# Attention with a threshold mask, followed by an MLP: keys and queries transposed in float32 before they are split in two, not after

## The chip, the cores and the metric

The kernel runs on one core of a Trainium2 chip. The metric is the device time of one execution in microseconds (us). A core has a matrix engine (TensorE, PE in the profile, with its weight loads as PEld), a vector engine (VectorE, DVE), an engine for activation functions and copies (ScalarE, ACT), a general engine (GpSimd, POOL) and an engine that here issues all transfers (SyncE, SP). Each engine runs its own instructions in a fixed order and waits for the others by semaphores.

## The reference

```python
def _attn_ref(q, k, v, tau):                       # 8 batches, 8 heads, 576 tokens, 64 dims
    scores = scale * np.matmul(q, k.transpose(0, 1, 3, 2))
    thresh = np.max(scores, axis=-1, keepdims=True) - tau
    scores = np.where(scores >= thresh, scores, -1000000000.0)
    attn = np.exp(scores - np.max(scores, axis=-1, keepdims=True))
    attn = attn / (np.sum(attn, axis=-1, keepdims=True) + 1e-09)
    return np.matmul(attn, v).astype(np.float32)

def _moe_ref(x, w_in, w_out):                      # x: 4608 tokens x 512, d_ff 2048
    h = x @ w_in
    g = np.maximum(h, 0.0) + np.log1p(np.exp(-np.abs(h)))      # softplus
    return (g @ w_out).astype(np.float32)
```

The heads of the attention's output are put side by side (8 x 64 = 512) and go through the MLP. The two weight matrices arrive in float64.

## The kernel before, in words

**Two halves of a number.** Matrix products are made in a shorter float format, `fp32r`. Every operand is split in two: `hi`, the value rounded to `fp32r` (`hi_of`), and `lo`, what is left of it (`lo_of`, a subtraction; L124). A product is then made of three or four products of halves. Much of what POOL, ACT and DVE do is this splitting.

**Units and tiles.** The attention goes by units of one head pair of one batch. A tile is 128 query rows of one head against its 576 keys; tile `M` holds the last 64 rows of both heads. Batches 1 to 7 have four units of nine tiles each (kind "all", 28 units). Batch 0 is cut into units of four tiles (kind "one") and of five (kind "two"), so that the MLP can begin early; there are eight of these. In all there are 36 units and 288 tiles. For a tile the steps are: scores (L391), row maximum on DVE (L397), exponential on ACT (L405), mask and row sum on DVE (L410), transposes of the masked weights `e_all` on PE (L441), their hi copy on ACT (L462) and lo on DVE (L124, `gL`), and the product with the values (L485 and after).

**What prepares a unit.** While a unit's tiles run, the steps of `pre` make the next unit ready; `ST` (and `STEPS` for batch 0) says at which tile each is called. Before the change these are: `split_k` and `split_q` make hi and lo of the loaded keys and queries on POOL (L117 hi, L124 lo), side by side as 128 columns, 64 of hi and 64 of lo. `qkT` transposes each block of 128 tokens in `fp32r` on PE (L336 for the eight whole blocks of the two heads, L328 and L330 for the last 64 tokens), so that one transpose gives hi on 64 partitions and lo on the other 64. ACT copies the results from PSUM: `kT` (L340), `qT` with the scale (L349), the rest (L358, L364). Two transfers on SP make `qT` with its halves swapped (L353, L354). A score product is `kT` with `qT` plus `kT` with the swapped `qT`, which gives all four products of halves. `split_v` makes the values' halves on POOL (`vt`).

**The MLP.** It runs in chunks of tokens between the attention's tiles, one chunk of 512 tokens to a batch, as single matmuls that fill TensorE's queue: hidden layer `h` (L574, L576, L578), softplus on ACT (L596, `st`), hi on DVE (L121, `g`) and lo on POOL (L124, `g<-st,g`), output `o` (L632, L634, L636; the last takes the lo half). Sixteen blocks `g_<chunk>_<block>` make a chunk. After the last tile, at about 1340 us, only the MLP is left.

**The weights.** In batch 0 and after it the float64 weights are loaded, decoded with integer operations on DVE (six for a block, L172 to L184), two on ACT and one on POOL (L189), and the decoded `w_in` goes to a store in HBM. There are 32 blocks.

**What sets the order.** The program calls each tile's steps by a fixed pattern, a planner's list of late calls (`defer`, `point`) puts copies a step or two behind, and a scheduler then fixes the order of each engine's instructions. All transfers are on SP's queue.

## Time and profile before

| | |
|---|---|
| median of 3 runs | 1544.3 us (1540.53 to 1549.28) |
| profiled execution: its time / its span | 1545.64 us / 1543.5 us |
| mean granted TensorE clock | 0.966 |
| PE, PEld busy | 91%, 78% of the span |
| DVE, ACT, POOL busy | 70%, 59%, 38% |
| work only in the MLP | from about 1340 us |

The page divides the span into busy shares and follows back the chain of work that ended last. The first 250 us, in which the weights are decoded, and the time behind them differ in what they wait for, so the table's shares are to be read by stretches of time. Of an operation the page gives its line, its engine, the names of its tiles (out<-in), its partitions by elements, its count, its total busy time and the mean of one in ns, and behind the second bar the idle time of the engine just ahead of it, with what ended it.

### The profile page before, as it was taken

To read this page: it belongs to the slowest core of one execution; us is meant where nothing else is said; L and a number is where in the kernel's file an instruction comes from. 1 tells how busy PE (TensorE), PEld (TensorE's weight loads), DVE (VectorE), ACT (ScalarE), POOL (GpSimd) and SP (SyncE) were. 2 spreads that over 40 slices of the span, in tenths; PEclk is the share of its full clock that TensorE was granted. 3 is DMA by queue.
4 is the path that set the end of the run, shared out by engine and by line. 5 is a ranking of instruction groups with operands and counts; after the bars stand their busy time and mean duration, and the time that the engine had idled before them with its cause. 6 is when DMAs were issued, how large, how long until landed. Compare 5 with 4: busy or idle time off the path is not lost.

```text
span 1543.5 us, 24467 instructions
## 1 busy us (share of the span) xinstructions
PE 1410.7 (91%) x8076; PEld 1202.7 (78%) x8076; DVE 1073.9 (70%) x2372; ACT 917.8 (59%) x1861; POOL 588.1 (38%) x612
## 2 busy tenths in 40 slices
PE   4555778889899999999999999999999999999998
PEld 4444767778788888888888888888888888878887
DVE  7999798778777777777777777777777777511212
ACT  5565676677576657666776576666666666511110
POOL 4554445334243334334433433344334332242321
PEclk9776899999999999999999999999999999999999
DMA  6767764544343355434443353335334532352331
GB/s 171 217 184 207 244 204 133 172 132 127 106 126 113 108 130 144 116 112 118 149 115 104 100 160 102 108 110 147 111 106 114 146 105 77 101 173 96 118 101 41
DMA packets 142030, 202.44 MB, mean 131 GB/s; under 512 B 38192, under 2 KB 97872, under 8 KB 141904
## 3 DMA queue, kind: packets, MB, share of 16 engines
q1 hardware_dynamic: 141904, 200.89, 44.6%
q8 instruction: 64, 1.05, 0.3%
q14 instruction: 62, 0.51, 0.1%
HBM read 152.44 MB, written 27.41 MB: 117 GB/s over the span
## 4 chain that ended last, share of the span: by engine, by line
PE 61%; ACT 10%; DVE 8%; issue 4%; DMA 3%; POOL 2%; SPq 1%; POOLq 0%; ACTq 0%; DVEq 0%
PE s L391 8%; PE o L636 6%; PE o L632 6%; PE o L634 6%; PE h L574 6%; PE s L441 6%; PE h L576 6%; PE h L578 6%; PE pv L485 3%; PE pv L486 3%; ACT L596 2%; DVE e_all L410 2%; ACT gH L462 2%; ACT st L596 2%; ACT L405 1%
## 5 line engine op out<-in xcount | busy, mean ns | idle before, releaser
L124 POOL TENSOR_TENSOR g<-st,g 128x512 fp32r<-128x512 f32 x144 | 193.2, 1359 | 206.3 <-DVE g L121 206.3
L410 DVE SCALAR_TENSOR_TENSOR e_all<-s,thr,e_all 128x576 f32<-128x576 f32 x288 | 234.7, 816 | 34.8 <-ACT e_all L405 29.6
L576 PE MATMUL h<-xl,wi 128*128 128x512 f32 (+1 forms) x640 | 246.4, 385 | 0.0
L574 PE MATMUL h<-xh,wi 128*128 128x512 f32 (+1 forms) x640 | 244.4, 382 | 1.1 <-DMA wi<-wi_d 0.5
L578 PE MATMUL h<-xh,wi 128*128 128x512 f32 (+1 forms) x640 | 242.8, 379 | 0.0
L397 DVE TENSOR_REDUCE negm<-s 128x1 f32<-128x576 f32 x288 | 216.9, 754 | 29.6 <-PE s L391 25.6
L636 PE MATMUL o<-wo_o,g 128*128 128x512 f32 x576 | 231.6, 402 | 4.9 <-POOL g L124 4.9
L632 PE MATMUL o<-wo_o,g 128*128 128x512 f32 x576 | 233.5, 405 | 1.7 <-ACT st L596 1.4
L634 PE MATMUL o<-wo_o,g 128*128 128x512 f32 x576 | 229.6, 399 | 0.0
L405 ACT ACTIVATE e_all<-s,negm 128x576 f32<-128x576 f32 x288 | 214.0, 743 | 7.8 <-DVE negm L397 5.9
L391 PE MATMUL s<-kT,qT 128*128 128x288 f32 x1024 | 201.1, 317 | 5.1 <-DMA qT<-qT 2.1
L124 DVE TENSOR_TENSOR gL<-s,gH 128x512 fp32r<-128x512 f32 (+1 forms) x240 | 150.2, 634 | 74.5 <-ACT gH L465 38.9
L462 ACT CAST gH<-s 128x512 fp32r<-128x512 f32 (+1 forms) x240 | 129.0, 550 | 120.5 <-PE s L446 65.6
L391 PEld LDWEIGHTS s<-kT,qT 128*128 128x128 f32 x1024 | 153.6, 196 | 23.8 <-DVE gH L124 14.7
L121 DVE CAST g<-st 128x512 fp32r<-128x512 f32 x144 | 67.0, 502 | 149.5 <-ACT st L596 148.9
L485 PE MATMUL pv<-gH,vt 128*128 128x320 f32 (+1 forms) x512 | 148.4, 310 | 1.4 <-ACT gH L462 1.4
L596 ACT ACTIVATE st<-h 128x512 f32<-128x512 f32 x144 | 78.5, 596 | 117.8 <-PE h L578 117.1
L486 PE MATMUL pv<-gL,vt 128*128 128x320 f32 (+1 forms) x512 | 146.1, 305 | 0.0
L574 PEld LDWEIGHTS h<-xh,wi 128*128 128x128 f32 x640 | 123.9, 194 | 22.5 <-ACT gH L462 0.7
L441 PE MATMUL s<-identr,e_all 128*128 128x128 f32 x864 | 135.2, 279 | 6.9 <-DVE e_all L410 5.9
L578 PEld LDWEIGHTS h<-xh,wi 128*128 128x128 f32 x640 | 123.2, 193 | 19.4
L576 PEld LDWEIGHTS h<-xl,wi 128*128 128x128 f32 x640 | 123.8, 193 | 18.6
(107 smaller groups left out, 2558.9 us busy)
## 6 DMA issues: line engine op xcount, KB each, us to landing
wi<-wi_d SPq DMA_DIRECT2D x160, 512.0 KB
qT<-qT SPq DMA_DIRECT2D x112, 128.0 KB
kn<-in_k_dram SPq DMA_DIRECT2D x36, 256.0 KB
qn<-in_q_dram SPq DMA_DIRECT2D x36, 256.0 KB
vn<-in_v_dram SPq DMA_DIRECT2D x36, 256.0 KB
wc_i<-in_moe_w_in_dram SPq DMA_DIRECT2D x16, 512.0 KB
wc_o<-in_moe_w_out_dram SPq DMA_DIRECT2D x16, 512.0 KB
R<-r_d SPq DMA_DIRECT2D x56, 144.0 KB
```

Source lines behind the costliest of these rows:

```text
L124: eng.tensor_tensor(out=out_, in0=in_, in1=hi.bitcast(F32), op=ALU.subtract)
L391: nc.tensor.matmul(sp[:, hf, 0:HS], lhs, s.kT[j][:, k0 + hf * HS:k0 + (hf + 1) * HS], start=(m == 0), stop=(m == len(parts) - 1))
L397: nc.vector.reduce_max(negm, s.sp[t][:, :, 0:HS], axis=AX.XY, negate=True)
L405: nc.scalar.activation(e_all[:, s.half[t], :].rearrange("p (h n) -> p h n", h=2), s.sp[t][:, :, 0:HS], AF.Exp, bias=s.m[t][0], scale=1.0)
L410: nc.vector.scalar_tensor_tensor(out=e2, in0=s.sp[t][:, :, 0:HS], scalar=s.m.pop(t)[1], in1=e2, op0=ALU.is_ge, op1=ALU.mult, accum_out=s.s ...
L441: nc.tensor.transpose(main[:, c, :], e[:, c0:c0 + P], ident)
L574: nc.tensor.matmul(h, wi[:, 0, cc, :], u.h[cc], start=(cc == 0), stop=False)
L576: nc.tensor.matmul(h, wi[:, 0, cc, :], u.l[cc], start=False, stop=False)
L578: nc.tensor.matmul(h, wi[:, 1, cc, :], u.h[cc], start=False, stop=(cc == NCC - 1))
L632: nc.tensor.matmul(o, gh[:, sl], wo[fc][:, 0, :], start=(i == 0), stop=False)
L634: nc.tensor.matmul(o, gh[:, sl], wo[fc][:, 1, :], start=False, stop=False)
L636: nc.tensor.matmul(o, gl[:, sl], wo[fc][:, 0, :], start=False, stop=(i == QF - 1))
```

## The change

Keys and queries go to TensorE as they were loaded, in float32. One transpose takes two blocks of 64 columns, which are two of the four token blocks of a head (`pair_T`), so the eight whole blocks of a head pair need four transposes for keys and four for queries, with the identity read as float32. The last 64 tokens of both heads, keys in 64 partitions and queries in the others, are loaded into a tile of their own, `rn`, and share one transpose (`rest_T`). The result has no halves yet: on partitions 0 to 63 stand the columns of one token block, on 64 to 127 those of the other.

In unit 0 ACT makes hi and DVE lo directly from PSUM (`pair_parts`). In every other unit (`pair_raw`) ACT copies the raw values, 128x256 of keys and 128x256 of queries (128x128 in batch 0's "one" and "two"), into the tile `raw`, and POOL makes hi and lo from it, each on 64 partitions: for each head two hi and two lo of `kT`, and two of each for `qT`. The lo goes to the other 64 partitions, as a score product needs it. The rests are copied to `rr` by ACT and split by POOL in the same way (`rest_raw`, `rest_parts`), with those for tile `M` in `qm`. The swapping transfers follow POOL's last instruction. The steps of `pre` become six and are called later in the unit: tiles 3, 4, 4, 5, 6 and 8 in place of 1, 3, 4, 4, 5, 6, 6 and 8. Transposes of keys and queries fall from 648 to 308 (19 to 9 for a unit "all"); POOL's instructions rise from 617 to 944, SP's fall from 923 to 823 and ACT's from 1704 to 1673.

```diff
-ST = (1, 3, 4, 4, 5, 6, 6, 8)
+ST = (3, 4, 4, 5, 6, 8)
...
+RAW = ("all", "one", "two")
...
+                s.cc = (slice(0, 2), slice(0, 1), slice(1, 2))[("all", "one", "two").index(kind)]
...
+        s.rn = apool.tile([P, 2, D], F32, tag="rn", bufs=2, name=f"rn_{s.i}")
+        for n, (t, src) in enumerate(((s.kn, k), (s.qn, q))):
             load_rows(s, t, src)
-            if t is s.qn and s.kind == "one":
-                continue
-            for j in range(2):
-                nc.sync.dma_start(t[j * SR:(j + 1) * SR, NC, :], src[s.b, h0 + j, SM:S, :])
+            nc.sync.dma_start(s.rn[n * SR:(n + 1) * SR], src[s.b, h0:h0 + 2, SM:S, :].rearrange("h p d -> p h d"))
+        s.kT, s.qT, s.vt = [], [], []
...
-    def split_k(s):
-        s.k2 = apool.tile([P, 9, 2 * D], F32R, tag="k2", bufs=1, name=f"k2_{s.i}")
-        hi_of(s.eng, s.k2[:, :, 0:D], s.kn[:, 0:9, :])
-        lo_of(s.eng_lo, s.k2[:, :, D:2 * D], s.kn[:, 0:9, :], s.k2[:, :, 0:D])
-        s.q2, s.kT, s.qT, s.vt = [], [], [], []
-    def split_q(s, j):
-        t = apool.tile([P, NC + 1, 2 * D], F32R, tag="q2", bufs=1, name=f"q2_{s.i}_{j}")
-        a, z = s.cols.start, s.cols.stop
-        if j == 0 and s.kind != "one":
-            z += 1
-        qj = s.qn[:, j * (NC + 1) + a:j * (NC + 1) + z, :]
-        hi_of(s.eng, t[:, a:z, 0:D], qj)
-        lo_of(s.eng_lo, t[:, a:z, D:2 * D], qj, t[:, a:z, 0:D])
-        s.q2.append(t)
...
-    def qkT(s, j, n):
-        ps = ps_g.tile([P, 512], F32, tag="g", name=f"tr_{s.i}_{j}_{n}")
-        pr = ps.bitcast(F32R)
-        if n == 2:
-            nc.tensor.transpose(pr[:, 0:P], s.k2[:, NC, :], identr)
-            if j == 0 and s.kind != "one":
-                nc.tensor.transpose(pr[:, P:2 * P], s.q2[0][:, NC, :], identr)
-            defer(1, lambda: qkT_rest(s, j, ps))
-            return
-        cols = range(NC) if n == 0 else range(NC)[s.cols]
-        for c in cols:
-            src = s.k2[:, j * (NC + 1) + c, :] if n == 0 else s.q2[j][:, c, :]
-            nc.tensor.transpose(pr[:, c * P:(c + 1) * P], src, identr)
-        if n == 0:
-            s.kT.append(apool.tile([P, S + SR], F32R, tag="kT", name=f"kT_{s.i}_{j}"))
-            t = s.kT[j]
-            defer(1, lambda: nc.scalar.copy(t[:, SR:S], ps))
-        else:
-            t = [apool.tile([P, SM], F32R, tag=f"qT{i}", name=f"qT{i}_{s.i}_{j}") for i in range(2)]
-            s.qT.append(t)
-            w = slice(cols[0] * P, (cols[-1] + 1) * P)
-            defer(1, lambda: queries(t[0][:, w], t[1][:, w], ps[:, w]))
-    def queries(t0, t1, ps):
-        nc.scalar.activation(t0, ps, AF.Copy, scale=qscale)
-        swap(t0, t1)
-    def swap(t0, t1):
-        nc.sync.dma_start(t1[0:D].bitcast(F32), t0[D:P].bitcast(F32))
-        nc.sync.dma_start(t1[D:P].bitcast(F32), t0[0:D].bitcast(F32))
-    def qkT_rest(s, j, ps):
-        nc.scalar.copy(
-            s.kT[j].rearrange("p (k n) -> p k n", n=SR)[:, 0:NC * 2 + 2:NC * 2 + 1, :],
-            ps[:, j * SR:(j + 1) * SR].unsqueeze(1).to_broadcast([P, 2, SR]),
-        )
+    def pair_T(s, j):
+        ps = ps_g.tile([P, 4, P], F32, tag="g", name=f"tr_{s.i}_{j}")
+        for i, t in enumerate((s.kn, s.qn)):
+            for c in range(2) if i == 0 else range(2)[s.cc]:
+                a = (j * (NC + 1) + 2 * c) * D
+                nc.tensor.transpose(ps[:, 2 * i + c, :], t.rearrange("p s d -> p (s d)")[:, a:a + P], ident)
+        s.kT.append(apool.tile([P, S + SR], F32R, tag="kT", name=f"kT_{s.i}_{j}"))
+        s.qT.append([apool.tile([P, SM], F32R, tag=f"qT{i}", name=f"qT{i}_{s.i}_{j}") for i in range(2)])
+        defer(1, lambda: pair_raw(s, j, ps) if s.i and s.kind in RAW else pair_parts(s, j, ps))
+    def blocks(t, c, o):
+        return t.rearrange("p (c o n) -> p c o n", o=2, n=P)[:, c, o, :]
+    def half(i):
+        return slice(i * D, (i + 1) * D)
+    def pair_raw(s, j, ps):
+        t = apool.tile([P, 4, P], F32, tag="raw", bufs=1, name=f"raw_{s.i}_{j}")
+        nc.scalar.copy(t[:, 0:2, :], ps[:, 0:2, :])
+        q_ = slice(2 + s.cc.start, 2 + s.cc.stop)
+        nc.scalar.activation(t[:, q_, :], ps[:, q_, :], AF.Copy, scale=qscale)
+        for i, c, to in ((0, slice(0, 2), s.kT[j][:, SR:S]), (2, s.cc, s.qT[j][0])):
+            for o in range(2):
+                src = t[half(o), i + c.start:i + c.stop, :]
+                hi = blocks(to[half(o)], c, o)
+                hi_of(nc.gpsimd, hi, src)
+                lo_of(nc.gpsimd, blocks(to[half(1 - o)], c, o), src, hi)
+        swap(s, j)
+    def pair_parts(s, j, ps):
+        t0 = s.qT[j][0]
+        for o in range(2):
+            src = ps[half(o), 2 + s.cc.start:2 + s.cc.stop, :]
+            hi = blocks(t0[half(o)], s.cc, o)
+            nc.scalar.activation(hi, src, AF.Copy, scale=qscale[half(o)])
+            nc.vector.scalar_tensor_tensor(out=blocks(t0[half(1 - o)], s.cc, o), in0=src, scalar=qscale[half(o)],
+                                           in1=hi.bitcast(F32), op0=ALU.mult, op1=ALU.subtract)
+        swap(s, j)
+        for o in range(2):
+            src = ps[half(o), 0:2, :]
+            to = s.kT[j][:, SR:S]
+            hi = blocks(to[half(o)], slice(0, 2), o)
+            nc.scalar.copy(hi, src)
+            lo_of(nc.vector, blocks(to[half(1 - o)], slice(0, 2), o), src, hi)
+    def swap(s, j):
+        t0, t1 = s.qT[j]
+        w = slice(s.cols.start * P, s.cols.stop * P)
+        for o in range(2):
+            nc.sync.dma_start(t1[half(o), w].bitcast(F32), t0[half(1 - o), w].bitcast(F32))
+    def rest_T(s):
+        ps = ps_g.tile([P, 512], F32, tag="g", name=f"re_{s.i}")
+        nc.tensor.transpose(ps[:, 0:P], s.rn.rearrange("p h d -> p (h d)"), ident)
+        s.rr = apool.tile([P, P], F32, tag="rr", bufs=1, name=f"rr_{s.i}")
+        defer(1, lambda: rest_raw(s, ps))
+    def rest_raw(s, ps):
+        nc.scalar.copy(s.rr[:, 0:SR], ps[:, 0:SR])
+        nc.scalar.activation(s.rr[:, SR:P], ps[:, SR:P], AF.Copy, scale=qscale)
+        defer(1, lambda: rest_parts(s, 0))
+    def rest_parts(s, j):
+        def sides(t):
+            return t.rearrange("p (k n) -> p k n", n=SR)[:, 0:NC * 2 + 2:NC * 2 + 1, :]
+        src = s.rr[half(j), 0:SR].unsqueeze(1).to_broadcast([D, 2, SR])
+        hi = sides(s.kT[j][half(j)])
+        hi_of(nc.gpsimd, hi, src)
+        lo_of(nc.gpsimd, sides(s.kT[j][half(1 - j)]), src, hi)
         if j == 0 and s.kind != "one":
             for m in range(2):
-                nc.scalar.activation(qm[:, 0, m, m * SR:(m + 1) * SR], ps[:, P + m * SR:P + (m + 1) * SR],
-                                     AF.Copy, scale=qscale)
-            swap(qm[:, 0], qm[:, 1])
+                src, w = s.rr[half(m), SR:P], half(m)
+                hi = qm[half(m), 0, m, w]
+                hi_of(nc.gpsimd, hi, src)
+                lo_of(nc.gpsimd, qm[half(1 - m), 0, m, w], src, hi)
+            for o in range(2):
+                nc.sync.dma_start(qm[half(o), 1].bitcast(F32), qm[half(1 - o), 0].bitcast(F32))
...
-    def pre(s, first_):
-        def a():
-            split_k(s)
-        def b():
-            split_q(s, 0)
-            qkT(s, 0, 0)
-        def c():
-            qkT(s, 0, 1)
-            split_v(s, 0)
-        def d():
-            split_v(s, 1)
-            split_q(s, 1)
-        return [a, b, lambda: qkT(s, 0, 2), c, d, lambda: qkT(s, 1, 0), lambda: qkT(s, 1, 1),
-                lambda: qkT(s, 1, 2)]
-    STEPS = {
-        ("all", "all"): ST,
-        ("one", "one"): (0, 0, 0, 1, 1, 2, 2, 3),
-        ("one", "two"): (0, 0, 0, 1, 1, 2, 2, 3),
-        ("two", "two"): (0, 0, 1, 1, 2, 3, 3, 4),
-        ("two", "one"): (0, 0, 1, 1, 2, 3, 3, 4),
-        ("two", "all"): (0, 0, 1, 1, 2, 3, 4, 9),
-    }
+    def pre(s):
+        return [lambda: pair_T(s, 0), lambda: rest_T(s), lambda: split_v(s, 0), lambda: split_v(s, 1),
+                lambda: pair_T(s, 1), lambda: rest_parts(s, 1)]
+    STEPS = {"all": ST, "one": (0, 0, 1, 1, 2, 3), "two": (1, 1, 2, 2, 3, 4)}
...
-    eng, u0.eng, u0.eng_lo = u0.eng, nc.scalar, nc.vector
-    split_k(u0)
-    split_q(u0, 0)
-    for n in (0, 2, 1):
-        qkT(u0, 0, n)
-        point()
+    pair_T(u0, 0)
+    rest_T(u0)
+    point()
     load_v(u0)
     load(units[1])
-    split_q(u0, 1)
-    for n in (0, 2, 1):
-        qkT(u0, 1, n)
-        point()
-    u0.eng, u0.eng_lo = eng, nc.gpsimd
+    pair_T(u0, 1)
+    point()
+    rest_parts(u0, 1)
```

How the order moves on two engines, first on POOL where unit 29's keys and queries are prepared, around the lo halves of the MLP's blocks `g_5_14` and `g_5_15`. Before:

```order
L522 TENSOR_TENSOR xp_11522<-xp_11522,R_11950 128x576
L124 TENSOR_TENSOR g_5_14_12043<-st_14_12032,g_5_14_12042 128x512
L124 TENSOR_TENSOR g_5_15_12047<-st_15_12030,g_5_15_12046 128x512
L117 TENSOR_SCALAR q_29_1_12175<-qn_11849 128x4x64
L124 TENSOR_TENSOR xl_2_12212<-xst_2_12094,xh_2_12211 128x512
L124 TENSOR_TENSOR q_29_1_12175<-qn_11849,q_29_1_12175 128x4x64
```

With the change (`raw_0` and `rr` are ACT's raw copies, `kT_0` and `qT_29_0` the unit's transposed keys and queries):

```order
L550 TENSOR_TENSOR xp_11588<-xp_11588,R_12018 128x576
L125 TENSOR_SCALAR kT_0_12124<-raw_0_12131 64x2x128 x2
L132 TENSOR_TENSOR kT_0_12124<-raw_0_12131,kT_0_12124 64x2x128
L132 TENSOR_TENSOR g_5_14_12111<-st_14_12100,g_5_14_12110 128x512
L132 TENSOR_TENSOR g_5_15_12115<-st_15_12098,g_5_15_12114 128x512
L132 TENSOR_TENSOR kT_0_12124<-raw_0_12131,kT_0_12124 64x2x128
L125 TENSOR_SCALAR qT_29_0_12125<-raw_0_12131 64x2x128 x2
L132 TENSOR_TENSOR qT_29_0_12125<-raw_0_12131,qT_29_0_12125 64x2x128 x2
L125 TENSOR_SCALAR kT_0_12124<-rr_12188 64x2x64
```

Two hi and one lo of `kT_0` now stand between `xp` and `g_5_14`, where nothing stood. The same is found in the chunks 2, 3, 4 and 6.

The same engine in batch 0, where unit 2 (kind "one") is prepared. Before:

```order
L117 TENSOR_SCALAR q_2_0_457<-qn_400 128x2x64
L124 TENSOR_TENSOR q_2_0_457<-qn_400,q_2_0_457 128x2x64
L117 TENSOR_SCALAR k_2_454<-kn_399 128x9x64
L124 TENSOR_TENSOR k_2_454<-kn_399,k_2_454 128x9x64
L117 TENSOR_SCALAR vt_0_517<-vn_405 128x5x64
L124 TENSOR_TENSOR vt_0_517<-vn_405,vt_0_517 128x5x64
L189 TENSOR_TENSOR wa_i_2_413<-wa_i_2_413 128x512
L117 TENSOR_SCALAR q_2_1_523<-qn_400 128x2x64
L124 TENSOR_TENSOR q_2_1_523<-qn_400,q_2_1_523 128x2x64
L117 TENSOR_SCALAR vt_1_520<-vn_405 128x5x64
L124 TENSOR_TENSOR vt_1_520<-vn_405,vt_1_520 128x5x64
```

With the change:

```order
L125 TENSOR_SCALAR vt_0_528<-vn_411 128x5x64
L132 TENSOR_TENSOR vt_0_528<-vn_411,vt_0_528 128x5x64
L125 TENSOR_SCALAR kT_0_463<-raw_0_482 64x2x128 x2
L132 TENSOR_TENSOR kT_0_463<-raw_0_482,kT_0_463 64x2x128 x2
L125 TENSOR_SCALAR qT_2_0_464<-raw_0_482 64x128 x2
L132 TENSOR_TENSOR qT_2_0_464<-raw_0_482,qT_2_0_464 64x128 x2
L125 TENSOR_SCALAR kT_0_463<-rr_468 64x2x64
L132 TENSOR_TENSOR kT_0_463<-rr_468,kT_0_463 64x2x64
L125 TENSOR_SCALAR kT_1_589<-rr_468 64x2x64
L132 TENSOR_TENSOR kT_1_589<-rr_468,kT_1_589 64x2x64
L197 TENSOR_TENSOR wa_i_2_419<-wa_i_2_419 128x512
L125 TENSOR_SCALAR vt_1_531<-vn_411 128x5x64
```

Before, two instructions split the keys of both heads and two the queries of a head. With the change one head's keys and queries take eight and the last keys of both heads four, all behind the values `vt_0`; the other head's eight follow further down. `wa_i` is a block of weights.

On TensorE at unit 29's preparation, with the MLP's `o` matmuls between them. Before:

```order
L636 MATMUL o_3_0_12026<-wo_o_2518,g_5_14_12043 128x512
L632 MATMUL o_3_0_12026<-wo_o_2593,g_5_15_12046 128x512
L634 MATMUL o_3_0_12026<-wo_o_2593,g_5_15_12046 128x512
L636 MATMUL o_3_0_12026<-wo_o_2593,g_5_15_12047 128x512
L634 MATMUL o_3_1_12097<-wo_o_2373,g_5_13_11716 128x512
L636 MATMUL o_3_1_12097<-wo_o_2373,g_5_13_11717 128x512
L632 MATMUL o_3_1_12097<-wo_o_2518,g_5_14_12042 128x512
L328 MATMUL tr_0_2_12107<-identr,k_29_11940 128x128
L330 MATMUL tr_0_2_12107<-identr,q_29_0_12051 128x128
L336 MATMUL tr_0_1_12110<-identr,q_29_0_12051 128x128 x4
```

With the change:

```order
L664 MATMUL o_3_0_12094<-wo_o_2549,g_5_14_12111 128x512
L660 MATMUL o_3_0_12094<-wo_o_2630,g_5_15_12114 128x512
L662 MATMUL o_3_0_12094<-wo_o_2630,g_5_15_12114 128x512
L664 MATMUL o_3_0_12094<-wo_o_2630,g_5_15_12115 128x512
L662 MATMUL o_3_1_12176<-wo_o_2387,g_5_13_11785 128x512
L664 MATMUL o_3_1_12176<-wo_o_2387,g_5_13_11786 128x512
L660 MATMUL o_3_1_12176<-wo_o_2549,g_5_14_12110 128x512
L370 MATMUL re_12186<-identr,rn_11923 128x128
L419 MATMUL s_141<-kT_1_11827,qT_28_1_11828 128x288 x2
```

One transpose of `rn` stands where there were one of the last keys, one of the last queries and four of the queries; the first head's queries are transposed earlier, two at a time, together with its keys.

11 lines of the change are left out of this document (2 added, 9 removed).

## The prediction

> **What bounds the kernel now.** I read the page's busy shares and slices first, then the busy time by stretches, to learn where a saved microsecond of an engine counts. The columns of the second fence are start and end, length, then busy time and count on PE, PEld, DVE, ACT and POOL, granted clock, DMA share and GB/s.
>
> ```profile
> PE 1410.7 (91%) x8076; PEld 1202.7 (78%) x8076; DVE 1073.9 (70%) x2372; ACT 917.8 (59%) x1861; POOL 588.1 (38%) x612
> PE   4555778889899999999999999999999999999998
> DVE  7999798778777777777777777777777777511212
> ```
>
> ```profile
> 0.00:250.00 250.00, 152.74 (x896) 137.67 (x897) 222.42 (x443) 161.32 (x360) 127.03 (x146) 0.81 0.66 201
> 32.00:51.00 19.00, 11.44 (x73) 9.91 (x71) 17.54 (x39) 13.40 (x33) 10.79 (x15) 0.84 0.70 201
> 74.00:98.00 24.00, 11.86 (x73) 10.71 (x72) 23.45 (x45) 16.79 (x40) 13.86 (x18) 0.74 0.53 161
> 250.00:400.00 150.00, 134.74 (x915) 118.31 (x913) 113.67 (x249) 105.14 (x242) 56.44 (x63) 0.99 0.48 135
> 900.00:950.00 50.00, 49.77 (x292) 42.12 (x291) 36.23 (x84) 36.07 (x68) 19.35 (x20) 1.00 0.39 116
> ```
>
> Two regimes show. From 250 us on PE bounds: it is busy for 49.77 of 50 us at 900, with DVE and ACT at 36 and POOL at 19. In the first 250 us PE is busy for 153 and DVE for 222, because DVE decodes weights beside the masks of batch 0. So fewer transposes pay only in the 28 units "all" behind it, and what slows DVE costs in front.
>
> **PE's transposes.** The groups give a transpose's own duration; as PE overlaps matmuls, what one costs is the spacing in the chain of waits (start, time on the chain, instructions).
>
> ```profile
> L336 PE MATMUL tr<-identr,k 128*128 128x128 f32 x288 | 35.9, 252 | 9.9 <-DVE identr L94 6.9 <-POOL k L124 2.9
> L441 PE MATMUL s<-identr,e_all 128*128 128x128 f32 x864 | 135.2, 279 | 6.9 <-DVE e_all L410 5.9
> ```
>
> ```profile
> 904.21 0.44 PE s L441 x4
> ...
> 916.78 0.29 PE tr L336 x4
> ...
> 920.47 0.06 PE tr L328
> 920.53 0.06 PE tr L330
> 920.59 0.08 PE tr L336
> ...
> 921.34 0.20 PE tr L336 x3
> ```
>
> Four `fp32r` transposes take 0.28 to 0.29 us, 0.07 each, and those of the rests 0.06. The new ones read float32 with the float32 identity, as those of `e_all` do: 0.44 for four, 0.11 each. Per unit before: four groups of four, 2x0.29 + 2x0.28, and three rests, 3x0.06, make 1.32 us for 19. After: 9x0.11 = 0.99. That is 0.33 us a unit, and 28 units make **-9.2 us**. Half as many transposes at 1.6 times the price save a quarter of their time, not half. Bounds: -5 if batch 1 is still held by DVE and a fresh float32 transpose costs 0.12, -12 if it costs 0.10.
>
> **The lo of the MLP's g.** POOL's queue is where the change adds most, so I looked at where PE waits for POOL now: before `o` L636, whose lo half POOL makes.
>
> ```profile
> L124 POOL TENSOR_TENSOR g<-st,g 128x512 fp32r<-128x512 f32 x144 | 193.2, 1359 | 206.3 <-DVE g L121 206.3
> L636 PE MATMUL o<-wo_o,g 128*128 128x512 f32 x576 | 231.6, 402 | 4.9 <-POOL g L124 4.9
> ```
>
> Most of `g` has slack: POOL idles ahead of it and PE's idle time before L636 is 4.9 us in all. In each chunk one pair has none. This is the place of the order fence, in a chunk near 1040 us (start, duration, engine, line, operation, tile; in brackets the idle time before).
>
> ```profile
> 1035.44 1.43 POOL L522 TENSOR_TENSOR xp<-xp,R 128x576 f32<-128x576 f32 x1 [1.54 <-DMA R<-r_d]
> ...
> 1036.66 1.09 ACT L596 ACTIVATE st<-h 128x512 f32<-128x512 f32 x2
> ...
> 1037.64 0.59 ACT L340 CAST kT<-tr 128x512 fp32r<-128x512 f32 x1
> ...
> 1038.29 2.64 POOL L124 TENSOR_TENSOR g<-st,g 128x512 fp32r<-128x512 f32 x2 [1.42 <-DVE g L121]
> ...
> 1039.74 0.50 PE L636 MATMUL o<-wo_o,g 128*128 128x512 f32 x1 [0.51 <-POOL g L124]
> ...
> 1040.98 0.50 PE L636 MATMUL o<-wo_o,g 128*128 128x512 f32 x1 [0.27 <-POOL g L124]
> ```
>
> ```profile
> L117 POOL TENSOR_SCALAR q<-qn 128x256 fp32r<-128x256 f32 x28 | 11.4, 407 | 25.2 <-PE tr L336 24.7
> L124 POOL TENSOR_TENSOR q<-qn,q 128x256 fp32r<-128x256 f32 x28 | 20.7, 738 | 1.9
> L117 POOL TENSOR_SCALAR q<-qn 128x128 fp32r<-128x128 f32 x10 | 3.5, 346 | 15.9 <-PE tr L336 15.8
> L124 POOL TENSOR_TENSOR q<-qn,q 128x128 fp32r<-128x128 f32 x10 | 4.7, 471 | 0.8
> L462 ACT CAST gH<-tm 128x256 fp32r<-128x256 f32 x16 | 5.2, 375 | 7.2 <-PE tm L441 7.2
> ```
>
> POOL sits idle for 1.42 us ahead of these `g`, and PE already waits for them. In the new order two hi and one lo of `kT_0` come between. They need ACT's raw copy, which takes the place of the `kT` copy at 1037.64: 128x256 instead of 128x512, so 0.38 us, to 1038.02. POOL then does 2x0.407 + 0.738 = 1.55 us and begins `g` at 1039.57 instead of 1038.29: 1.28 us later, and PE with it. Five chunks have this order: **+6.4 us**. I price the 64-partition operations by their columns, not their elements: no row has 64 partitions on POOL, and 256 against 128 columns is 738 against 471. Bounds: 0, if the copy comes sooner because the transposes no longer wait for a split; 5x2.3 = 11.5, if the second lo and the scheduler's other pairs are in the way as well.
>
> **DVE's decoding beside a busier POOL.** POOL's load per unit: "one" had 0.721 + 1.490 for keys and 2x(0.346 + 0.471) for queries, 3.85 us.
>
> ```profile
> L117 POOL TENSOR_SCALAR k<-kn 128x576 fp32r<-128x576 f32 x35 | 25.2, 721 | 158.9 <-PE tr L328 158.8
> L124 POOL TENSOR_TENSOR k<-kn,k 128x576 fp32r<-128x576 f32 x35 | 52.1, 1490 | 2.7
> L189 POOL TENSOR_TENSOR wa_i<-wa_i 128x512 fp32r<-128x512 f32 x16 | 21.3, 1333 | 10.8 <-DVE wa_i L184 4.2 <-ACT e_all L405 3.6 <-ACT thr L399 3.0
> ```
>
> Now it has 4x(0.407 + 0.738) for keys, 4x(0.346 + 0.471) for queries and half as much, 1.63, for the rests: 9.5 us, 5.6 more. "Two" gains some 7, with the two pairs for `qm`. Three units of "one" and four of "two" (unit 0 takes the other path) make about 42 us on POOL's 127 of the first 250 us. Does DVE feel it? The same decode operation on the same size:
>
> ```profile
> 13.28 1.93 POOL L124 TENSOR_TENSOR k<-kn,k 128x576 fp32r<-128x576 f32 x1
> ...
> 13.97 1.52 DVE L184 TENSOR_SCALAR wa_i<-wb_i 128x512 uint32<-128x512 uint32 x1
> ...
> 27.77 0.42 DVE L184 TENSOR_SCALAR wa_i<-wb_i 128x512 uint32<-128x512 uint32 x1
> ```
>
> ```profile
> L184 DVE TENSOR_SCALAR wa_o<-wb_o 128x512 uint32<-128x512 uint32 x13 | 8.5, 656 | 0.1
> L184 DVE TENSOR_SCALAR wa_i<-wb_i 128x512 uint32<-128x512 uint32 x16 | 8.3, 519 | 0.0
> ```
>
> Under POOL's subtraction it took 1.52 us and ended behind it, without one 0.42. The mean excess is 0.10 and 0.24 us in the two groups, 4.7 us for 29 blocks; six such kinds of operation make 28 us now. Scaled by 42/127 that is 9.3 us, of which DVE's busy share there, 0.89, reaches the end: **+8 us**. Bounds: 0, if the new operations fall into its waits; for the top, 42 us times the share of time in which DVE decodes, 192 operations at some 0.6 us or nearly half of 250, 20 us. The Trainium skill says in "SBUF — State Buffer" (two separate sides) that GpSimd and certain DVE operations, those with two SBUF inputs among them, lock a shared port pair for a whole instruction, and the other blocks. The 1.52 us agrees with it; taken for every overlap, the rule would put the bound of 20 in the sum, where the means of the groups speak for 8.
>
> **What costs nothing.** ACT copies less per unit and bounds nowhere (36 of 50 us, 161 of 250), so I count no gain. POOL's 7.7 us more per unit "all" lie in its idle 31 of 50 us, except at the `g` above; without that cover they would show as PE waiting before `o`. Unit 0 makes its parts on ACT and DVE with no split ahead of the transposes; its eight short DVE operations replace two long ones while the first weights are awaited, and I call it even, within 1.5 us. On SP the waits of the loads for `k2`'s buffers go:
>
> ```profile
> SPq L286 <- POOL k L124: 143.6, 26, 8.2
> ```
>
> but the two swapping transfers now wait for POOL's last lo of the queries, and behind them in SP's order stand the loads of the MLP's weights `wi`, which have three buffers. A unit "all" calls its last `pair_T` at tile 6 of 9, with two tiles of time; I count nothing. In batch 0 the units are shorter and the margin is thin, which is a rival.
>
> **The sum.** -9.2 + 6.4 + 8 = +5.2 us on the profiled 1545.6 (span 1543.5) gives 1550.8. The profiled run lies 1.3 above the median of 1544.3, so 1549.5 for a median: **1549 us**, no change. About 0.5% (7.7 us) is what a measurement of this kernel can tell from none. The likeliest case's own range is 1541 to 1558.
>
> **Rivals.** *Faster.* The `kT` copies come early enough, or the hi of `g` late enough, that POOL's wait costs nothing, and decoding does not feel the new operations. For it: the 206 us of idle time ahead of `g`, and new work that is spread over the unit. Against: it waits at that very place and PE behind it. Only the transposes remain: 1545.6 - 9.2 - 1.3 = 1535 us.
>
> *Slower: POOL ends last in batch 0.* In the two stretches quoted POOL works 10.79 of 19 us ("one") and 13.86 of 24 ("two"); with 5.6 and 7 more it is at 16.4 of 19 and 21 of 24, in an order fixed ahead, with waits for ACT's raw copies, for DVE's decoded blocks (L189, 1.333 us each) and for values. The second head's eight instructions follow all these; when two blocks or so stand ahead of them, keys and queries are 2.7 us late, PE's first scores of the next unit wait, and DVE with them. It decides from the point where POOL's work with its waits passes the unit's length. Seven units make 19 us: 1549.5 + 19 = 1568 us. Against: 86% is not full.
>
> *A transpose costs its whole duration.* "TensorE: Matmul & The Clock Gate" (Part 4) of the Trainium skill gives about 275 ns for a transpose in context, mostly latency, which would make their number count. By this case's rows that is 28x(19x0.252 - 9x0.279) = 64 us, and 1549.5 - 64 + 9 = 1495 us. The spacing of 0.06 to 0.11 us in the chain speaks against it.
>
> **Chances.** No change 0.38; faster 0.31 and whole durations 0.04, so 0.35 faster; POOL's lateness 0.27 slower, as it takes little to use up a thin margin. The range runs from between the fast case and the one below it to the slow one with the decode bound: 1526 to 1570.
>
> **What would show it.** Right: the chain has four float32 transposes at 0.44 us; POOL starts those `g` over a us later and PE's idle time before `o` L636 <- POOL grows from 5 to about 11 us; decode operations on DVE grow by some 30% of their excess and batch 0 ends 8 us later. Wrong: PE waits for `kT` or `qT` before scores L391 in units 1 to 8 (POOL's lateness); no growth before `o` (the fast case); spacing of 0.25 us per transpose.

## The result, and the profile after

| | before | changed |
|---|---|---|
| median | 1542.4 us (1540.4 to 1549.3, 4 runs) | 1591.4 us (1589.0 to 1593.5, 4 runs) |
| ratio | | 1.0309, 95% interval 1.0271 to 1.0347 |
| span of the profiled run | 1543.5 us | 1587.1 us |
| mean granted TensorE clock | 0.966 | 0.945 |

The change makes the kernel 3.1% slower, 49 us. The forecast was no change, 1549 us, with a range up to 1570. The two profiled runs, in which the places below are read, took 1545.64 and 1588.98 us, so they show 43 of the 49 us; the rest is spread between runs and is not placed.

Where it goes is read from the first mask of each unit, taken from the order of the mask operations on DVE (us from the span's start):

| first mask of unit | 1 | 2 | 4 | 6 | 8 | 13 | 21 | 29 | 35 |
|---|---|---|---|---|---|---|---|---|---|
| before | 34.1 | 54.7 | 103.3 | 163.5 | 231.8 | 419.5 | 738.5 | 1059.4 | 1299.8 |
| changed | 35.0 | 62.2 | 119.0 | 192.7 | 275.1 | 465.7 | 783.2 | 1103.8 | 1344.1 |
| later by | 0.9 | 7.5 | 15.7 | 29.3 | 43.3 | 46.3 | 44.7 | 44.5 | 44.3 |

The whole loss lies in batch 0 (units 0 to 7) and the first units behind it: 43.3 us by unit 8, of which unit 8 itself wins 4.9 back (40.0 us instead of 44.9), and 7.8 us more in units 9 to 12 (150.7 us instead of 142.9). From unit 13 on nothing is lost and a little is won: a chunk of four units takes 160.3 us instead of 160.4 (three chunks from unit 20 to unit 32).

The page's busy shares of the changed kernel, and its stretches (columns as in the prediction):

```profile
PE 1408.9 (89%) x7736; PEld 1189.3 (75%) x7736; DVE 1093.2 (69%) x2377; ACT 880.1 (55%) x1798; POOL 838.0 (53%) x1234
```

```profile
0.00:250.00 250.00, 132.93 (x677) 118.69 (x677) 204.82 (x389) 133.21 (x308) 161.19 (x247) 0.74 0.60 176
900.00:950.00 50.00, 47.90 (x268) 40.30 (x267) 37.70 (x87) 26.48 (x57) 26.05 (x40) 0.97 0.43 119
```

POOL has 838 us of work instead of 588, in 1234 instructions instead of 612 by the two pages; the count of 944 given with the change is too low. In the first 250 us it is busy for 161, not 127, and DVE, which bound that stretch with 222 us, is busy for only 205: it has work and doesn't get to it. What it waits for stands in the waits of DVE in the first 275 us (total, times, longest), before:

```profile
DVE negm L397 <- PE s L391: 7.4, 7, 3.7
DVE wa_i L172 <- DMA wc_i<-in_moe_w_in_dram: 3.9, 1, 3.9
```

and in the changed kernel, with SP's longest wait of the same stretch:

```profile
DVE wa_o L180 <- DMA wc_o<-in_moe_w_out_dram: 14.5, 8, 4.5
DVE wa_i L180 <- DMA wc_i<-in_moe_w_in_dram: 10.3, 4, 4.1
```

```profile
SPq L365 <- POOL qT L132: 76.9, 17, 8.3
```

DVE now waits 24.8 us for weights to be decoded, where it was 4.4 before, and SP stands for 76.9 us in front of the swapping transfers, until POOL has made its last lo of the queries (before the change the longest sum there was 14.4 us, for ACT's copy). A place where the two meet, from the timeline of the changed kernel:

```profile
99.14 0.60 SPq L290 DMA_DIRECT2D rn<-in_q_dram  x1
...
103.32 0.98 POOL L132 TENSOR_TENSOR qT<-raw,qT 64x128 fp32r<-64x128 f32 x2
103.80 1.16 SPq L365 DMA_DIRECT2D qT<-qT  x2
...
106.86 1.10 SPq L394 DMA_DIRECT2D qm<-qm  x2
...
108.01 0.58 SPq L171 DMA_DIRECT2D wc_o<-in_moe_w_out_dram  x1
...
112.04 0.85 DVE L180 TENSOR_SCALAR wa_o<-wc_o 128x512 uint32<-128x512 uint32 x1 [2.14 <-DMA wc_o<-in_moe_w_out_dram]
```

SP's last free issue is at 99.14. It then waits for `qT`, waits again for `qm`, and only at 108.01 issues the load of the next block of weights, which has nothing to do with POOL. DVE stands at 112.04 for that block.

Two more shares are seen in the groups of the changed kernel's first 275 us. POOL's own operations and the decoding:

```profile
L132 POOL TENSOR_TENSOR kT<-raw,kT 64x256 fp32r<-64x256 f32 x32 | 25.9, 810 | 2.5
L184 DVE TENSOR_SCALAR wa_i<-wa_i 128x512 f32<-128x512 f32 x16 | 11.7, 732 | 0.9 <-ACT wa_i L179 0.9
L185 DVE TENSOR_SCALAR wa_i<-wa_i 128x512 uint32<-128x512 uint32 x16 | 10.7, 667 | 0.0
```

Before the change the two decode operations took 626 and 526 ns:

```profile
L176 DVE TENSOR_SCALAR wa_i<-wa_i 128x512 f32<-128x512 f32 x16 | 10.0, 626 | 0.0
L177 DVE TENSOR_SCALAR wa_i<-wa_i 128x512 uint32<-128x512 uint32 x16 | 8.4, 526 | 0.0
```

Summed over all decode operations up to unit 8's first mask, each counted from the end of the one before it on DVE, DVE spends 115.9 us instead of 103.5. Up to there DVE's books close: of the 43.3 us it is idle for 24.6 more, 20.4 of them for weights, and busy for 18.8 more, 12.4 of them on decoding.

Behind batch 0 the predicted wait is there, at the lo of the MLP's `g` (timeline of the changed kernel):

```profile
917.72 1.43 POOL L550 TENSOR_TENSOR xp<-xp,R 128x576 f32<-128x576 f32 x1 [1.78 <-DMA R<-r_d]
...
920.15 0.94 POOL L125 TENSOR_SCALAR kT<-raw 64x256 fp32r<-64x256 f32 x2 [1.01 <-ACT raw L334]
921.17 0.72 POOL L132 TENSOR_TENSOR kT<-raw,kT 64x256 fp32r<-64x256 f32 x1
921.97 2.50 POOL L132 TENSOR_TENSOR g<-st,g 128x512 fp32r<-128x512 f32 x2
...
923.28 0.50 PE L664 MATMUL o<-wo_o,g 128*128 128x512 f32 x1 [2.00 <-POOL g L132]
```

```profile
L664 PE MATMUL o<-wo_o,g 128*128 128x512 f32 x576 | 235.1, 408 | 11.8 <-POOL g L132 11.7
```

PE's idle time there went from 4.9 to 11.7 us, and four of the new transposes in a row take 0.44 us on the chain:

```profile
961.28 0.44 PE tr L321 x4
```

### The profile page after: what moved, and what is told of

It reads as the page before. It is cut to its first block, busy times and chain, and to the rows that moved or that the text cites. A ratio compares the mean times of both kernels' runs of the same rounds, so it can differ in the third digit from the quotient of the medians.

```text
span 1587.1 us, 24497 instructions
## 1 busy us (share of the span) xinstructions
PE 1408.9 (89%) x7736; PEld 1189.3 (75%) x7736; DVE 1093.2 (69%) x2377; ACT 880.1 (55%) x1798; POOL 838.0 (53%) x1234
## 4 chain that ended last, share of the span: by engine, by line
PE 65%; ACT 9%; DVE 6%; issue 3%; DMA 3%; POOL 3%; SPq 1%; POOLq 0%; ACTq 0%; DVEq 0%
PE s L419 9%; PE o L664 7%; PE o L662 7%; PE o L660 7%; PE s L469 6%; PE h L604 6%; PE h L602 6%; PE h L606 6%; PE pv L514 4%; PE pv L513 4%; DVE e_all L438 2%; ACT gH L490 2%; ACT e_all L433 2%; ACT L624 1%; ACT L433 1%
## 5 line engine op out<-in xcount | busy, mean ns | idle before, releaser
L132 POOL TENSOR_TENSOR g<-st,g 128x512 fp32r<-128x512 f32 x144 | 187.9, 1324 | 155.2 <-DVE g L129 153.8
L664 PE MATMUL o<-wo_o,g 128*128 128x512 f32 x576 | 235.1, 408 | 11.8 <-POOL g L132 11.7
L660 PE MATMUL o<-wo_o,g 128*128 128x512 f32 x576 | 234.5, 407 | 2.9 <-ACT st L624 1.2
L662 PE MATMUL o<-wo_o,g 128*128 128x512 f32 x576 | 233.4, 405 | 0.0
L419 PE MATMUL s<-kT,qT 128*128 128x288 f32 x1024 | 206.9, 325 | 24.6 <-DVE kT L132 8.3
L132 DVE TENSOR_TENSOR gL<-s,gH 128x512 fp32r<-128x512 f32 (+1 forms) x240 | 150.6, 636 | 89.1 <-ACT gH L493 54.1
L419 PEld LDWEIGHTS s<-kT,qT 128*128 128x128 f32 x1024 | 158.5, 203 | 55.2 <-DVE gH L132 18.2
L129 DVE CAST g<-st 128x512 fp32r<-128x512 f32 x144 | 71.8, 534 | 143.9 <-ACT st L624 143.0
L550 POOL TENSOR_TENSOR xp<-xp,R 128x576 f32<-128x576 f32 (+2 forms) x36 | 47.4, 1317 | 203.6 <-DMA R<-r_d 196.7
L514 PE MATMUL pv<-gL,vt 128*128 128x320 f32 (+1 forms) x512 | 150.6, 313 | 0.0
L469 PE MATMUL tm<-identr,e_all 128*128 128x128 f32 x288 | 56.5, 330 | 102.4 <-DVE e_all L438 99.3
L602 PEld LDWEIGHTS h<-xh,wi 128*128 128x128 f32 x640 | 123.4, 193 | 25.1 <-DVE gH L132 2.7
L664 PEld LDWEIGHTS o<-wo_o,g 128*128 128x128 f32 x576 | 110.7, 192 | 36.2 <-POOL g L132 17.5
```

Source lines behind the costliest of these rows:

```text
L132: eng.tensor_tensor(out=out_, in0=in_, in1=hi.bitcast(F32), op=ALU.subtract)
L419: nc.tensor.matmul(sp[:, hf, 0:HS], lhs, s.kT[j][:, k0 + hf * HS:k0 + (hf + 1) * HS], start=(m == 0), stop=(m == len(parts) - 1))
L602: nc.tensor.matmul(h, wi[:, 0, cc, :], u.h[cc], start=(cc == 0), stop=False)
L660: nc.tensor.matmul(o, gh[:, sl], wo[fc][:, 0, :], start=(i == 0), stop=False)
L662: nc.tensor.matmul(o, gh[:, sl], wo[fc][:, 1, :], start=False, stop=False)
L664: nc.tensor.matmul(o, gl[:, sl], wo[fc][:, 0, :], start=False, stop=(i == QF - 1))
```

## The experiments

Three theories stood against each other for batch 0. S: transfers that wait for POOL hold SP's queue, and the weight loads behind them come late. C: POOL's added work slows DVE's decoding. L: keys and queries are late, and PE waits for them. All times are medians beside the kernel before on the same chip.

**Old preparation in batch 0, new behind it.**

```diff
-RAW = ("all", "one", "two")
+RAW = ("all",)
+OLD = ("one", "two")
...
+        if s.kind in OLD:
+            return pre_old(s)
```

`pre_old` is the preparation of the kernel before. To hold both kinds, this run and those that are new from unit 13 keep the last tokens in `kn` and the raw copies in the tiles of the old halves, `q2` and `k2`, and load the whole blocks side by side, so their units "all" are not the changed kernel's in every buffer.

> Edit: batch 0's eight units get the old preparation (split on POOL, then fp32r transposes), the 28 units of batches 1 to 7 the new one. The two traces show the whole loss by the start of batch 1 (unit 8's first mask at 275.1 instead of 231.8 us) and equal chunks behind it (160.2 against 160.4 us). If the loss is a matter of batch 0 alone, unit 8 starts near 232 us and the time is 1542 +- 6 us. The rival, that POOL's added work in batches 1 to 7 costs as well, says 1555 us or more.

Measured: 1560.5 us against 1543.2, ratio 1.0104 (1.0081 to 1.0127). The time lies in the rival's range, but the work added in batches 2 to 7 is not what costs it. Up to unit 7 every unit stands where it stood before (202.8 against 203.1 us), so batch 0's loss is gone; but 9.8 us are lost while unit 7, of five tiles, prepares unit 8 the new way, and 16.9 by unit 13. Behind it 2 us are won back. The first part lies beside the last decoding, which here ends at 260 us. The second does not: units 9 to 12 take 150.6 us, as in the changed kernel (150.7; before 142.9), from 286 to 436 us.

**New preparation from unit 13 on.**

```diff
+N0 = 13
...
+        if s.i < N0:
+            return pre_old(s)
```

> Edit: units 0 to 12 (batches 0 and 1 and the first of batch 2) prepared the old way, units 13 to 35 the new way, steps as in the change. With old batch 0 alone the units up to 7 took what they took before, and 17 us were lost from unit 8 to unit 13; from unit 13 on five chunks gained 0.4 each. If that loss lies in the first units of the new kind beside the last decoding, it goes: 1541 us, 2 us under before (23 units by 0.33 us of PE less five waits before the MLP's g of a microsecond). If it is the price of the passage from old to new, 1550 us or more.

Measured: 1543.7 us against 1543.8, ratio 1.000 (0.9986 to 1.0013). The 17 us of the run above are gone, so they were the price of units 8 to 12 there. What remains is the prediction's account of batches 2 to 7: the transposes' gain and the wait at `g` cancel.

**The weight loads out of SP's queue.**

```diff
-        nc.sync.dma_start(st, src.bitcast(U32))
+        nc.scalar.dma_start(st, src.bitcast(U32))
```

> Edit: the changed kernel, with the loads of the float64 weights (32 of 512 KB) issued by ACT's queue instead of SP's. Theory S (queue): the swapping transfers of qT wait on SP for POOL's last lo, 77 us in the first 275, and the weight loads stand behind them, so that DVE waits 25 us for weights; without them in that queue DVE's wait for weights falls below 6 us and the time by 15 to 25, to 1566 to 1576 us. Theory C (contention: decode operations slowed by POOL) and theory L (keys and queries late for the scores): no change, 1588 to 1593 us.

Measured: 1581.1 us, ratio 1.0234 (1.0206 to 1.0261), 10 us under the changed kernel; outside theory S's numbers, but not what C and L say either. DVE's wait for weights falls from 24.8 to 2.8 us, as S says. A part of it returns in another place (waits of DVE in the first 275 us):

```profile
DVE negm L425 <- PE s L419: 10.9, 10, 3.2
```

DVE waits for scores, 10.9 us instead of 1.6. PE's wait for keys and queries of POOL and of the swaps is nearly what it was, 11.2 us instead of 10.1 (20 us to unit 8), which suggests that what the wait for weights hid before now holds DVE up. The edit has a price of its own as well. ACT issues the first block of weights at 0.76 us, beside the first keys, where SP did so at 6.98, and unit 0's first mask comes at 23.2 us instead of 19.6. From there to unit 8's first mask 14.5 us are won.

**The same loads, earlier in SP's order.**

```diff
+        with tc.high_priority(400):
             nc.sync.dma_start(st, src.bitcast(U32))
```

> Edit: the changed kernel, the same loads on SP's queue but placed earlier in its order by a higher priority, so that five or six of the swapping transfers of batch 0 stand behind a load that they stood ahead of. Theory S: a part of the 25 us comes back, 5 to 15 us, to 1576 to 1586 us, and DVE's wait for weights falls with it. Theories C and L: 1588 to 1593 us.

Measured: 1579.8 us, ratio 1.0229 (1.0208 to 1.0250), as theory S says; DVE's wait for weights is 15.3 us. Here too the first block is loaded ahead of the keys, at 0.74 us, and unit 0's first mask comes at 23.3 us.

**The swaps issued by POOL.**

```diff
-            nc.sync.dma_start(t1[half(o), w].bitcast(F32), t0[half(1 - o), w].bitcast(F32))
+            (nc.gpsimd if s.i else nc.sync).dma_start(...)      # and the same for qm
```

> Edit: the changed kernel, with the swapping transfers of qT and qm (all units but the first) issued by POOL, straight behind its own last lo, instead of by SP. Theory S (queue): nothing on SP waits for POOL's lo, the weight loads and the MLP's loads of x run ahead, DVE's wait for weights falls from 25 us to below 6. Since the weight loads on ACT's queue gave only 10 us, with the scores then waiting for late keys, theories S and L together say 1573 to 1583 us. If each transfer costs POOL a microsecond or more of its own, POOL is later still and the time is 1590 us or more. Theory C alone: 1588 to 1593 us.

Measured: 1577.1 us, ratio 1.0221 (1.0201 to 1.0241). The time is in the range, its reason isn't: DVE's wait for weights is still 20.7 us. The waits of SP show why, and POOL's groups what an issue costs:

```profile
SPq L220 <- POOL wa_i L197: 35.8, 12, 6.3
SPq L554 <- POOL xp L550: 35.5, 4, 12.8
```

```profile
L365 POOL DMA_DIRECT2D qT<-qT x140 | 77.9, 557 | 0.1
```

SP has other transfers that wait for POOL, the stores of decoded weights and of `xp`; POOL, with 0.56 us for each transfer added, is later with these. Of the 14 us won in the profiled run, 6 lie ahead of unit 8 and most of the rest between units 9 and 14. Units 9 to 12 take 140.5 us, less than before the change (142.9), and in every run that leaves batch 1's new swaps on SP they take 150.6 to 151.9. So the second part of the loss, behind batch 0, is the price of these transfers on SP's queue.

**POOL's load alone.**

```diff
         s.q2.append(t)
+        if 0 < s.i < 8:
+            for _ in range(4 if j == 0 or s.kind == "two" else 3):
+                u_ = 2 if s.kind == "one" else 0
+                hi_of(nc.gpsimd, t[:, u_, :], ident)
+                lo_of(nc.gpsimd, t[:, u_ + 1, :], ident, t[:, u_, :])
```

> Edit: the kernel before, with idle work added on POOL in units 1 to 7: 53 pairs of a hi and a lo of 128x128, 0.346 + 0.471 us each, 43 us in all, into unused columns, which no other engine waits for. It is the change's added POOL load by itself, with the old split, transposes and transfers. Theory C (contention on DVE's decoding and POOL's own queue): decoding up by 8 to 13 us, the time by 8 to 20, to 1551 to 1563 us. Theory S: the swaps never wait for POOL here, so the weight loads stay early and DVE's wait for weights stays below 8 us; no more than 1550 us if contention is small.

Measured: 1554.5 us against 1543.8, ratio 1.0084 (1.0054 to 1.0115), theory C's number. Decoding up to unit 8 takes 115.1 us, 11.6 more than before; unit 8 is 12.7 us late; DVE's wait for weights is as before:

```profile
DVE wa_i L172 <- DMA wc_i<-in_moe_w_in_dram: 3.4, 1, 3.4
```

So POOL work that nobody waits for, priced at 43 us and 50 by the trace, costs 11 to 13 us, by slowing DVE: up to unit 8 DVE is busy for 13.2 us more and idle for no longer than before (26.1 us, 26.6 before). That is a quarter of batch 0's loss.

**Hi and lo from PSUM in batch 0, by ACT and DVE.**

```diff
-RAW = ("all", "one", "two")
+RAW = ("all",)
```

> Edit: in batch 0 hi is made by ACT and lo by DVE directly from PSUM, as unit 0 has it, instead of the raw copy and POOL; the rests stay on POOL. POOL loses some 65 of its 175 us there, DVE gets eight operations a unit, 2.5 to 2.8 us for each of seven units, 19 us. Theory C: decoding falls by some 8 of its 12.5 us of excess, DVE's own 19 us more than eat it, 1595 to 1602 us. Theory S: the swaps wait for DVE and ACT rather than for POOL's queue, DVE's wait for weights falls by 15 to 20 us, together 1575 to 1590 us.

Measured: 1582.3 us, ratio 1.0237 (1.0211 to 1.0264), inside theory S's range. Decoding is down to 106.8 us, DVE waits for weights 4.1 us and PE for keys not at all. Unit 8 is 27.3 us late, and the operations that DVE does for keys and queries take 24.5 us up to there, 3.1 of them unit 0's, which the changed kernel has too: with POOL unburdened (114.9 us of work up to there, 114.7 before the change) all three effects shrink to little or nothing, and most of what is left is what DVE does in its place.

**Keys earlier, with the weight loads on ACT's queue.**

```diff
-    ... "one": (0, 0, 1, 1, 2, 3), "two": (1, 1, 2, 2, 3, 4)}
+    ... "one": (0, 0, 2, 3, 1, 1), "two": (0, 0, 3, 4, 1, 2)}
```

> Edit: the changed kernel with the weight loads on ACT's queue (1581 us), and in batch 0 both pair_T and the rests called ahead of the values' halves, at tiles 0 and 1 (one) and 0, 1 and 2 (two). Theory L: with the weights' wait gone, PE waits 19 us before scores for late keys and queries (5 us in the changed kernel behind unit 0); earlier preparation takes 8 to 12 us of it, to 1569 to 1573 us, and what remains over before is contention (11 us) and the start. If the keys are late because POOL is behind in everything, moving the values behind them only makes the values late: 1578 to 1584 us.

Measured: 1586.8 us, ratio 1.0271 (1.0245 to 1.0296), 6 us worse than without it and above both answers. Unit 2 starts 4.5 us earlier behind unit 1, later units lose more (unit 3 to 4: 27.6 us instead of 24.3). In this order what is called sooner makes other things late, so the next run takes work off POOL.

**Less work on POOL, none of it to DVE.**

```diff
-                hi_of(nc.gpsimd, hi, src)
+                if s.kind == "all":
+                    hi_of(nc.gpsimd, hi, src)
+                elif i == 0:
+                    nc.scalar.copy(hi, ps[half(o), 0:2, :])
+                else:
+                    nc.scalar.activation(hi, ps[half(o), 2 + c.start:2 + c.stop, :], AF.Copy, scale=qscale[half(o)])
```

> Edit: the changed kernel, with batch 0's hi of kT and qT written by ACT straight from PSUM beside its raw copies; POOL makes only the lo there. POOL loses 60 of its instructions in batch 0, some 26 of 184 us, ACT gains as many (0.3 to 0.4 us each, 21 us, on 165 of 275 us). Theory that POOL's load in batch 0 is the common cause (it slows decoding, makes keys and queries late and holds the swaps back on SP): a third to a half of the 43 us, 12 to 20, comes back, to 1571 to 1579 us, with shorter waits of SP for qT and of DVE for weights, and decoding 3 to 5 us shorter. Rival, that ACT is as tight as POOL in batch 0: 1586 us or more.

Measured: 1577.1 us, ratio 1.0218 (1.0198 to 1.0238), 14 us under the changed kernel, as expected. PE's waits before the scores (20 to 262 us), changed kernel and this one:

```profile
L419 PE MATMUL s<-kT,qT 128*128 128x288 f32 x124 | 33.8, 403 | 10.2 <-POOL kT L132 5.7 <-POOL qT L132 4.4
```

```profile
L424 PE MATMUL s<-kT,qT 128*128 128x288 f32 x128 | 32.1, 379 | 1.8 <-DVE e_all L443 1.8
```

Keys are in time, the wait for weights falls to 16.8 us and decoding to 112.6, with POOL busy for 156 us up to unit 8 instead of 181.

> Edit: both, hi on ACT in batch 0 and the weight loads on ACT's queue. If late keys and the queue are two separate prices, the gains add: 10 us for the loads and what hi on ACT gave, 1561 to 1570 us. If the loads' wait only hid the wait for late keys, or is itself gone with the shorter split, the second gain is 3 us or less beside the first.

With the loads on ACT's queue as well it takes 1572.1 us, ratio 1.0188 (1.0168 to 1.0208). The second gain is 5 us, between the two answers. But here as well the loads on ACT delay the start: unit 0's first mask comes at 23.6 us instead of 19.5. Counted from that mask to unit 13's, the changed kernel takes 446.1 us, with the loads on ACT 437.0, with hi on ACT 436.0, with both 424.7. By these profiled runs the two gains, 9.1 and 10.1 us, add up (21.4); how far they overlap is not shown.

**The place of the wait at g.** Two runs on the kernel that is new from unit 13:

```diff
-ST = (3, 4, 4, 5, 6, 8)
+ST = (2, 4, 4, 5, 6, 8)
```

> Edit: as new from unit 13, with the first pair_T called at tile 2 instead of 3, which takes the hi and lo of kT_0 out from ahead of g_14 in POOL's order. The prediction's two terms for the MLP's stretch, -0.33 us a unit on PE and +1.28 us a chunk at g, say that only the first remains: 5 to 6.5 us under the run with step 3, 1535 us. If the g wait was not the price of that place, it is equal to it, 1541 us.

Measured: 1561.1 us against 1543.8, ratio 1.0111 (1.0088 to 1.0134): 17 us worse instead of 5 better; neither answer came. No new operation stands directly ahead of `g` in POOL's order, but eight stand a little further ahead, and POOL's timeline runs through without a gap:

```profile
877.42 2.53 POOL L134 TENSOR_TENSOR xl<-xst,xh 128x512 fp32r<-128x512 f32 x2 [6.31 <-ACT xh L129]
879.92 0.88 POOL L127 TENSOR_SCALAR kT<-q 64x256 fp32r<-64x256 f32 x2
...
883.47 1.82 POOL L134 TENSOR_TENSOR qT<-q,qT 64x256 fp32r<-64x256 f32 x2
885.37 1.47 POOL L627 TENSOR_TENSOR xp<-xp,R 128x576 f32<-128x576 f32 x1
886.80 2.49 POOL L134 TENSOR_TENSOR g<-st,g 128x512 fp32r<-128x512 f32 x2
```

So the wait at `g` does not go: what counts there is the sum of POOL's work since its last idle time, not the instruction next to `g`. It does not explain the 17 us, though. PE's idle time before `o` is 12.1 us, and 11.2 in the run with step 3. What grew is PE's wait before the scores, with step 3 and with step 2:

```profile
L496 PE MATMUL s<-kT,qT 128*128 128x288 f32 x1024 | 204.2, 321 | 10.8 <-DVE gL L134 6.1 <-DMA qT<-qT 3.4 <-DVE gH L134 0.3
L496 PE MATMUL s<-kT,qT 128*128 128x288 f32 x1024 | 203.7, 320 | 19.1 <-DVE gL L134 10.7 <-DVE gH L134 5.2 <-DMA qT<-qT 1.3
```

Between the first masks of units 13 and 35 the run is 16.0 us longer, and 13.2 us of it are waits before scores for DVE's lo of the weights, `gL` and `gH`. Why DVE is later with these was not taken apart.

```diff
-ST = (3, 4, 4, 5, 6, 8)
+ST = (4, 5, 4, 5, 6, 8)
```

> Edit: new from unit 13 on, with pair_T(s, 0) and rest_T called at tiles 4 and 5 instead of 3 and 4, so that in POOL's order kT_0, qT and the rests stand behind g_14 and g_15, with xl and xp alone ahead of them as before the change. In the run with step 2 eight of these operations stood ahead of xp and POOL reached g later still (wait before o 2.96 us, in the run with step 3 2.28, before the change 0.78). Theory of the two terms: the g wait falls back to about 1.3 us a chunk with it the slower o matmuls behind it, and 23 units save 0.33 us each: 5 to 8 us under before, 1535 to 1539 us, PE's idle time before o from POOL's g near 5 us. If POOL's later work falls behind and makes PE wait for kT or qT at the next unit, 1543 us or more.

Measured: 1535.2 us against 1542.8, ratio 0.9938 (0.9916 to 0.9960): 7.6 us faster, as expected. The new work stands behind `g`, POOL idles ahead of it again, and PE's idle time there is what it was before the change:

```profile
871.94 2.63 POOL L134 TENSOR_TENSOR g<-st,g 128x512 fp32r<-128x512 f32 x2 [2.65 <-DVE g L131]
```

```profile
L741 PE MATMUL o<-wo_o,g 128*128 128x512 f32 x576 | 232.2, 405 | 4.9 <-POOL g L134 4.9
```

**The same with the swaps issued by POOL from unit 13 on.**

```diff
-            nc.sync.dma_start(t1[half(o), w]...)
+            nc.gpsimd.dma_start(t1[half(o), w]...)        # and the same for qm
```

> Edit: the run with step 4, with the swapping transfers of units 13 and on issued by POOL instead of SP. With the swaps on POOL throughout, units 9 to 35 took 1018.7 us against 1029.1 in the changed kernel, most of it between units 9 and 14. Theory S: one wait for the MLP's x at the first units of the new kind goes, 1 to 4 us under the run with step 4. If POOL's own time for issuing matters, the same or up to 5 us over it.

Measured: 1527.1 us against 1542.8, ratio 0.9897 (0.9868 to 0.9927), 8 us under the run with step 4, more than expected, and 1% faster than the kernel before. In the profiled runs a chunk takes 158.0 us instead of 159.1, some 6 us over units 13 to 35; another 5 us lie ahead of unit 10, where both kernels do the same and profiled runs differ by as much, so part of the 8 us may not be the edit's. Why a chunk gains 1.1 us isn't shown by a single wait. A case of transfers waiting behind a swap on SP, in the changed kernel's chain of waits:

```profile
442.58 0.33 POOL qm L132
...
443.09 0.55 SPq L394
...
443.73 0.55 SPq L693
...
444.37 3.67 DMA xst<-x_d
```

The MLP's load of `xst` waits behind the swap of `qm`, and the chain follows it for the 3.67 us of its transfer; unit 12 takes 41.3 us instead of 37.1.

## Why the prediction was wrong

*PE's transposes, -9.2 us.* Right. The new ones take 0.11 us each in the chain. In the run with step 4, units 13 to 35 gain 8.2 us over 22 units, 0.37 each, against 0.33; that run changes more than the transposes, so it fits the size and does not isolate it.

*The lo of g, +6.4 us.* Right in place and nearly in size. POOL takes 0.47 us for a hi and 0.72 for a lo, priced at 0.41 and 0.74, and PE's idle time went from 4.9 to 11.7 us, where 5 to 11 was named. The price by columns held: 64x256 takes 0.737 us in the run with the swaps on POOL from unit 13 on, 128x256 took 0.738 before. The term is too small by what comes behind the wait: below.

*DVE's decoding, +8 us.* Right in mechanism, low in size: 12.4 us in the changed kernel, 11.6 with POOL's load alone. POOL's added work was set at 42 us, where its own figures, 3 x 5.6 and 4 x 7, make 45; up to unit 8 it has 181 us instead of 115, 66 more, through longer operations (0.810 us for a lo priced at 0.738), a longer stretch and unit 8's own preparation.

*SP, nothing.* This step failed. The prediction named what the swaps now wait for and that the MLP's loads stand behind them, but not the weight loads of batch 0, and it called the margin there thin without pricing it. 76.9 us of SP's waiting became 20.4 us more of DVE's waiting for weights; with the loads on another queue that wait is 2.8 us, and the time 10 us shorter. The loads of the MLP's input were also put at nothing, and in units 9 to 12 the new swaps on SP cost 10 us (150.7 against 140.5 with the swaps on POOL). SP's timeline has the weight loads behind the swaps, so the order of SP's instructions would have put the queue into the sum.

*The slower rival, 1568 us.* Its cause, POOL's length of work in batch 0, is the one that the runs bear out: with 25 us less on POOL (hi on ACT) decoding goes from 115.9 to 112.6 us, the wait for weights from 24.8 to 16.8, and no scores wait for keys. It was sized by one way of acting only, late keys at 2.7 us for seven units, and there PE waits 10.2 us before scores. The way by SP, which is twice that, was missing, and DVE's slowing was priced apart from it. The stretch from 74 to 98 us, read as a unit "two", lies in units 2 and 3, which are "one" (unit 4's first mask is at 103.3). 86% of POOL's time was read as not full; in the end it is busy for 66% of the time up to unit 8, and is late all the same. That its waits for ACT and for loads move all that stands behind them would explain this; no run isolates it.

*The other two rivals* fell: what the faster one expected at `g` didn't come, and the spacing of transposes stayed at 0.11 us.

*What would show it.* The sign named for POOL's lateness, PE waiting for `kT` or `qT` before scores in units 1 to 8, is there. No sign was named for SP.

What stays open: how much of the 43 us each way has for itself. POOL's load alone costs 11 to 13, the loads' place in the queue 10 to 12 with a start that is 4 us later, the hi operations 14, and how these overlap isn't shown. The 9.8 us at the passage from unit 7 to unit 8, with the old preparation in batch 0, weren't taken apart.
